# A top-k attention that feeds a mixture of experts: products moved inside the first 48 steps, and one row scaling a step

## The chip, the cores and the metric

The kernel runs on one core of a Trainium2 chip. The metric is the device time in microseconds (us) of one execution. PE is the matrix engine (TensorE), DVE the vector engine, ACT the scalar engine, POOL the GpSimd engine, SP the engine that issues most transfers. Each engine runs its own instructions strictly in order, and waits on the others by semaphores.

## What is computed

Eight batches of eight heads attend with 576 queries and keys of 64 numbers. In each row of scores only the 32 largest stay, the rest are masked. The rows of all heads (4608 x 512) then pass a mixture of eight experts, one expert to a token. All in float32; cut to what matters here:

```python
scores = scale * q @ k.T
kth = np.partition(scores, -32, axis=-1)[..., -32:-31]
scores = np.where(scores >= kth, scores, -1e9)
attn = np.exp(scores - scores.max(-1)); attn /= attn.sum(-1) + 1e-09
x = (attn @ v)                      # 4608 tokens x 512
e = argmax(x @ w_gate)              # one expert a token
out = gate_w * eom[e] * (relu(x @ w1[e]) @ w2[e])
```

## The kernel before

Attention is cut into 36 tiles of 128 queries and each tile into 4 steps of two heads: 144 steps. A step i is written as one pass of a loop (L873), and the order of the instructions on each engine is the order in which this loop writes them; nothing else sorts them. A pass works on several steps at once:

- PE: `scores(i+1)` (L275, into the PSUM tile `ps`), and the transposes of the exponentials of step i-2, `flip(i-2, part)` (L404, into PSUM tiles `pst`). A step has nine blocks of 128 columns. Part 0 is the first four (head 0), part 1 the fifth, which holds columns of both heads, part 2 the last four (head 1). `attend` (L436) multiplies them with the values, two steps at a time, in even passes.
- DVE: `rank` (L309, L312) finds 24 of the largest of step i from candidates, `window` (L351) the next eight of step i-1, `gmax` (L302) the candidates of step i+1, `choose` (L362, L366) the 32nd largest of step i-1, and `weigh` (L378) masks the exponentials of its head 0.
- ACT: a copy of the scores from PSUM (L283), `below` (L336, two sign functions, one to a head, which need the end of `rank`), `unveil` (L394, the exponential of head 1 of step i-2), copies of the transposes from PSUM (L412), `exps` (L346, head 0 of step i), and `veil` (L385, a sign function that needs `less`, L366).
- POOL: two sums after `below` (L339), which give `window` its input one pass later, `shift` (L325), and one sum after `veil` (L388).

In the first 48 steps (`LONE`) head 1 is masked by ACT and POOL (`veil`, `unveil`), in the later ones by DVE. There also run the slots of the mixture of experts (L714, L729), and after the last step a tail has the rest of them. In the first 48 steps PE has little to do, and 12 transposes of the identity without any use (L895) are written into each pass.

Once in four steps, when a tile is complete, two side products go through `side_start`: `gates` (L466, L457) in the passes with i mod 4 = 3, `rows` (L475, L457) in those with i mod 4 = 0. They share the PSUM tile of part 1, and are copied out after it (L470, L460). `rows` puts two scalings of the tile's rows on a list (L479, POOL); `run_slow(SUMS, ...)` starts those of cost 0.6 as long as the budget `SUMS` of a pass lasts. Small operations of the routing and of the setup are handed out one by one by `fill` (in the first steps the constants, L146 to L152). A pass with i mod 4 = 0 is called class 0 below, and so on to class 3; `attend` is in classes 0 and 2.

The pool `ps_t` has two banks in turn, so that a new tile `pst` waits until the last tile but one has been copied out.

Of the kernel before, what the change touches and what calls it, by code (L numbers as in the profile page):

```python
# [10 lines left out]
F32 = mybir.dt.float32  # L11
# [5 lines left out]
ALU = mybir.AluOpType  # L17
# [6 lines left out]
P = 128  # L24
# [5 lines left out]
USUAL = 11  # L30


SUMS = 1.3
DMAS = 2.0

NLIST = 12
# [3 lines left out]
def tile_topk_attention_moe(  # L40
# [11 lines left out]
    nc = tc.nc  # L52
# [77 lines left out]
    def setup():  # L130
# [5 lines left out]
        def gates():  # L136
            for a in range(2):
# [8 lines left out]
        ops = [lambda: nc.gpsimd.memset(wg, 0.0), gates,  # L146
               lambda: nc.gpsimd.memset(ones, 1.0), lambda: nc.gpsimd.memset(ones_b, 1.0),
               iota(before, [[1, P]], 0, -1),
               lambda: nc.gpsimd.tensor_scalar(before, before, 0.0, None, op0=ALU.is_gt),
               lambda: nc.vector.tensor_copy(before_b, before),  # L150
               iota(first, [[-1, E]], E), iota(carry0, [[REG, E]]),
               lambda: nc.gpsimd.memset(first_row, 0.0),  # L152
               iota(slot_iota, [[1, MAXS], [0, E]], 1), iota(slot_off, [[P, MAXS]]),
# [31 lines left out]
    def run(exact, stack):  # L185
# [205 lines left out]
        def unveil(i):  # L391
            if lone(i, 1):
                t, hp = divmod(i, NHP)
                nc.scalar.activation(EP[i][:, 1, :], VE.pop(i), AF.Exp, bias=VV.pop(i)[0][:, 1, 32:33], scale=SCALE,  # L394
                                     accum_out=SM[t][:, 2 * hp + 1:2 * hp + 2])

        def flip(i, part, extra=None):

            pt = EP[i].rearrange("p a s -> p (a s)")
            c0, c1 = ((0, 4), (4, 5), (5, 9))[part]  # L400
            n = c1 - c0
            ps = ps_t.tile([P, 4, P], F32, name="pst")
            for c in range(c0, c1):
                nc.tensor.transpose(ps[:, c - c0, :], pt[:, c * P:(c + 1) * P], ident)  # L404
            ev = extra(ps) if extra else None
            x = wk.tile([P, n, P], F32, name=f"pT{n}", bufs=6 if n == 4 else 3)
            PTT.setdefault(i, []).append(x)
            if part == 2:
                del EP[i]

            def copies():
                nc.scalar.activation(x, ps[:, :n, :], AF.Copy)  # L412
                if ev:
                    ev()
            return copies
# [398 lines left out]
        def side_start():  # L814

            f = side.popleft() if side else None

            def start(ps):
                copies, use = f(ps)
                uses.append(use)  # L820
                return copies
            return f and start

        def side_use():
            if uses:
                fill(len(urgent))
                uses.pop()()
# [45 lines left out]
        for i in range(NSTEP + 4):  # L873
            t, hp = divmod(i, NHP)
            step[0] = i
            if i + 1 < NSTEP:
                scores(i + 1)()
            for r in range(3):
                if i < NSTEP:
# [6 lines left out]
            spent[0] = 0.0  # L886
            if i < NSTEP:
                below(i)
            if 2 <= i < NSTEP + 2:
                unveil(i - 2)  # L890
            if 2 <= i < LONE:

                idle = ps_m.tile([P, 4, P], F32, name="pm")
                for c in range(12):
                    nc.tensor.transpose(idle[:, c % 4, :], ident, ident)  # L895
            early, late = [], []
            if 4 <= i < NSTEP + 4 and i % 2 == 0:
                early.append(attend(i - 4))
            if 2 <= i < NSTEP + 2:
                early.append(flip(i - 2, 0))  # L900
                early.append(flip(i - 2, 1, side_start()))
            if i >= NSTEP + 2:
                extra = side_start()
                if extra:
                    early.append(extra(ps_t.tile([P, 4, P], F32, name="pst")))
# [5 lines left out]
            if ev:  # L911
                late.append(ev)
            if 2 <= i < NSTEP + 2:
                late.append(flip(i - 2, 2))
            ev = turn_ahead() if room else None
            if ev:
                late.append(ev)
# [18 lines left out]
            run_slow(DMAS, ("ids", "out"))  # L936
            if 1 <= i <= NSTEP:
                veil(i - 1)
            side_use()
            fill(3)  # L940
            if i < NSTEP:
# [185 lines left out]
```

## Time and profile before

| | us |
|---|---|
| median of three runs (1297.45 to 1298.43) | 1297.87 |
| the profiled execution | 1299.58 |
| its span, first to last instruction | 1297.8 |
| steps 2 to 47 (22.70 to 342.71 of the span) | 320.0 |
| the later steps (342.71 to 1048.48) | 705.8 |
| the rest | 249.3 |

The profiled execution is 1.71 us above the median of the runs, and 1.8 us of its time lie outside the span. Stretches of the span are told by their start and end in us. A class is recognised in the trace by what follows: L475 marks class 0, L466 class 3. A step begins with the first L309 after L378.

### The profile page before, as it was taken

The numbers are of one execution on the slowest core, as the hardware profiler recorded it, in microseconds if no ns is written. First come the engines' busy times: TensorE is split into PE (matmuls) and PEld (weight loads), VectorE is DVE, ScalarE is ACT, GpSimd is POOL, SyncE is SP. The second block draws the span as 40 slices with busy tenths as digits, with TensorE's granted clock in tenths as the row PEclk, the third lists the DMA queues.
The fourth block names the chain that finished last, engine by engine and source line by source line (L and its number), as shares of the span: only waits on it lengthen the run. The fifth ranks groups of instructions, "written<-read, shape, count | busy, mean of one in ns | idle before, by whom it ended". The sixth has DMA issues, their size and how long they took to land.

```text
span 1297.8 us, 32273 instructions
## 1 busy us (share of the span) xinstructions
PE 1210.1 (93%) x10348; PEld 940.7 (72%) x10348; DVE 1143.7 (88%) x6113; ACT 984.5 (76%) x1928; POOL 758.2 (58%) x1221
## 2 busy tenths in 40 slices
PE   5887888887699999999999999999999999999996
PEld 4665665666577777777777777777777777999995
DVE  6999999999999999999999999999999963544443
ACT  5999998899887888888788787888887853454442
POOL 5666666588776766757667667567657733212110
PEclk7999999999999999999999999999999999999998
DMA  5400220021825654765456566755554467999990
GB/s 135 76 18 18 55 69 17 18 54 55 292 96 168 234 168 171 252 211 169 170 168 196 198 236 174 235 181 200 179 171 147 163 226 275 390 363 340 361 339 22
DMA packets 109387, 227.54 MB, mean 175 GB/s; under 512 B 14858, under 2 KB 33546, under 8 KB 108176
## 3 DMA queue, kind: packets, MB, share of 16 engines
q1 hardware_dynamic: 99536, 205.67, 47.6%
q0 software_dynamic: 7552, 18.96, 4.4%
q8 instruction: 86, 1.41, 0.5%
q10 hardware_dynamic: 2112, 0.68, 0.3%
q14 instruction: 101, 0.83, 0.2%
HBM read 206.68 MB, written 20.69 MB: 175 GB/s over the span
## 4 chain that ended last, share of the span: by engine, by line
PE 57%; DVE 24%; issue 14%; POOL 3%; ACT 1%; POOLq 0%; ACTq 0%
PE pm L714 14%; PE pm L729 13%; PE po L436 9%; PE ps L275 9%; PE pst L404 9%; DVE cand L302 8%; DVE v L351 5%; DVE cand L312 3%; DVE v L309 3%; DVE ep L378 2%; DVE x L362 2%; PE pst L457 1%; POOL xg L693 1%; PE pst L703 1%; PE pst L466 1%
## 5 line engine op out<-in xcount | busy, mean ns | idle before, releaser
L339 POOL TENSOR_TENSOR w<-s,marks 128x576 f32<-128x576 f32 x288 | 363.3, 1283 | 172.9 <-ACT marks L336 162.7
L302 DVE MAX8 cand<-s 128x8 f32<-128x72 f32 x2304 | 322.3, 222 | 8.7 <-ACT s L283 8.7
L714 PE MATMUL pm<-xs,w1t 128*128 128x128 f32 x2560 | 296.8, 275 | 0.9 <-issue 0.8
L714 PEld LDWEIGHTS pm<-xs,w1t 128*128 128x128 f32 x2560 | 292.0, 192 | 2.4 <-issue 1.1
L404 PE MATMUL pst<-ident,ep 128*128 128x128 f32 x1296 | 208.1, 285 | 68.7 <-ACT ep L394 56.2
L404 PEld LDWEIGHTS pst<-ident,ep 128*128 128x128 f32 x1296 | 148.6, 143 | 138.7 <-ACT ep L394 62.8
L336 ACT ACTIVATE marks<-s,v 128x576 int8<-128x576 f32 x288 | 220.9, 771 | 30.5 <-DVE v L309 27.2
L412 ACT ACTIVATE pT<-pst 128x512 f32<-128x512 f32 (+1 forms) x432 | 196.2, 484 | 17.0 <-PE pst L457 8.7
L351 DVE MAX8 v<-w 128x8 f32<-128x576 f32 x288 | 202.3, 745 | 0.0
L283 ACT ACTIVATE s<-ps 128x1152 f32<-128x1152 f32 (+1 forms) x145 | 163.2, 1126 | 51.5 <-PE ps L275 48.2
L275 PE MATMUL ps<-kst,qst 64*128 64x288 f32 (+1 forms) x1280 | 186.7, 442 | 5.4 <-ACT s L283 5.4
L378 DVE SCALAR_TENSOR_TENSOR ep<-s,kth,ep 128x576 f32<-128x576 f32 x240 | 188.7, 815 | 0.0
L436 PE MATMUL po<-pT,v 128*64 128x128 f32 (+3 forms) x3200 | 185.7, 267 | 0.1
L436 PEld LDWEIGHTS po<-pT,v 128*64 128x64 f32 (+1 forms) x3200 | 158.2, 136 | 33.8 <-issue 32.2
L729 PE MATMUL pm<-w2t,ht 128*128 128x512 f32 x400 | 180.4, 594 | 0.0
L346 ACT ACTIVATE ep<-s,v 128x576 f32<-128x576 f32 x240 | 176.1, 781 | 0.0
L740 POOL DMA_INDIRECT out_dram<-y,idt x40 | 49.8, 1246 | 190.9 <-ACT y L736 173.9
L309 DVE MAX8 v<-cand 128x8 f32<-128x64 f32 x864 | 148.4, 214 | 0.0
L275 PEld LDWEIGHTS ps<-kst,qst 64*128 64x128 f32 (+1 forms) x1280 | 100.7, 182 | 48.6 <-issue 25.1
L729 PEld LDWEIGHTS pm<-w2t,ht 128*128 128x128 f32 x400 | 72.2, 190 | 72.4 <-issue 72.4
L312 DVE MATCH_REPLACE8 cand<-v,cand 128x64 f32<-128x64 f32 x576 | 116.2, 210 | 0.0
L388 POOL TENSOR_TENSOR w<-s,marks 128x576 f32<-128x576 f32 x48 | 61.6, 1284 | 77.7 <-ACT marks L385 77.6
(166 smaller groups left out, 1520.9 us busy)
## 6 DMA issues: line engine op xcount, KB each, us to landing
w1t<-in_w_dram SPq DMA_DIRECT2D x40, 2048.0 KB
w2t<-in_w_dram SPq DMA_DIRECT2D x40, 2048.0 KB
v<-in_va_dram SPq DMA_DIRECT2D x8, 1152.0 KB
x_rows<-xu SPq DMA_DIRECT2D x36, 256.0 KB
qst<-in_qa_dram SPq DMA_DIRECT2D x70, 128.0 KB
kst<-in_ka_dram SPq DMA_DIRECT2D x14, 576.0 KB
ids<-far SPq DMA_DIRECT2D x1, 678.0 KB
xg<-x_rows,idt POOLq DMA_INDIRECT x40
```

What stands on the lines that cost most here:

```text
L275: nc.tensor.matmul(ps[qs, a, n, :288], Q[t][rows, hp, qs], K[b][rows, hp, cols], start=True, stop=True)
L302: nc.vector.max(out=c[:, 8 * g:8 * g + 8], in_=SC[i, a][:, g * GW:(g + 1) * GW])
L309: nc.vector.max(out=vs[:, a, 8 * r:8 * r + 8], in_=cs[a])
L336: nc.scalar.activation(m.bitcast(I8).rearrange("p (s b) -> p s b", b=2)[:, :, 1], s, AF.Sign, bias=vs[:, a, PIVOT - 1:PIVOT], scale=-(1.0 ...
L339: nc.gpsimd.tensor_tensor(w, s, m, op=ALU.add)
L351: nc.vector.max(out=VV[i][0][:, a, 24:32], in_=SW[i][0][a])
L378: nc.vector.scalar_tensor_tensor(e, SC.pop((i, a)), kth_col(i, a), e, op0=ALU.is_ge, op1=ALU.mult, accum_out=SM[t][:, 2 * hp + a:2 * hp + ...
L404: nc.tensor.transpose(ps[:, c - c0, :], pt[:, c * P:(c + 1) * P], ident)
L412: nc.scalar.activation(x, ps[:, :n, :], AF.Copy)
L436: nc.tensor.matmul(po[a * 64:(a + 1) * 64, k, qs], lhs, rhs, start=half and not k and not m, stop=(c == 3 and k == 1 and m == len(TT[t]) - 1))
L714: nc.tensor.matmul(ph[:, f - f0, :], w[:, c, f * P:(f + 1) * P], XS[s][:, c, :], start=(c == 0), stop=(c == NC - 1))
L729: nc.tensor.matmul(PY[s], HT[s][:, f, :], w[:, f, :], start=(f == 0), stop=(f == NF - 1))
```

## The change

In passes below 48 (`calm`), apart from a second version of the program for ties, which is not taken with these inputs:

- the scores are computed two steps ahead, not one: PE does them between part 1 and part 2 of the transposes, and ACT copies them after `veil`, at the end of the pass, ahead of the copy of part 2, which also moves there;
- part 0 is transposed first, and its copy stands ahead of `unveil`; then the side products, into the tile `mid`, in which part 1 later takes the first block; then `attend`, the 12 idle transposes, part 1, the scores, part 2.

In all passes the budget `SUMS` is 0.7, which lets one scaling of rows start in a pass, not two. In the setup, POOL writes the constant `before_b` itself, and a conversion on DVE goes.

```diff
-SUMS = 1.3
+SUMS = 0.7
 DMAS = 2.0
...
                iota(before, [[1, P]], 0, -1),
-               lambda: nc.gpsimd.tensor_scalar(before, before, 0.0, None, op0=ALU.is_gt),
-               lambda: nc.vector.tensor_copy(before_b, before),
+               lambda: nc.gpsimd.tensor_scalar(before_b, before, 0.0, None, op0=ALU.is_gt),
                iota(first, [[-1, E]], E), iota(carry0, [[REG, E]]),
                lambda: nc.gpsimd.memset(first_row, 0.0),
...
-        def flip(i, part, extra=None):
+        def flip(i, part, extra=None, bank=None):
             pt = EP[i].rearrange("p a s -> p (a s)")
             c0, c1 = ((0, 4), (4, 5), (5, 9))[part]
             n = c1 - c0
-            ps = ps_t.tile([P, 4, P], F32, name="pst")
+            ps = bank or ps_t.tile([P, 4, P], F32, name="pst")
             for c in range(c0, c1):
                 nc.tensor.transpose(ps[:, c - c0, :], pt[:, c * P:(c + 1) * P], ident)
-            ev = extra(ps) if extra else None
+            ev = extra(ps) if extra and not bank else extra
             x = wk.tile([P, n, P], F32, name=f"pT{n}", bufs=6 if n == 4 else 3)
             PTT.setdefault(i, []).append(x)
...
         for i in range(NSTEP + 4):
             t, hp = divmod(i, NHP)
             step[0] = i
-            if i + 1 < NSTEP:
+            if i + 1 < NSTEP and (i + 1, 0) not in SC:
                 scores(i + 1)()
             for r in range(3):
                 if i < NSTEP:
...
             spent[0] = 0.0
             if i < NSTEP:
                 below(i)
+            early, late, last = [], [], []
+            calm = i < LONE and not exact
+            mid = None
+            if calm and 2 <= i:
+                first_copy = flip(i - 2, 0)
+                mid = ps_t.tile([P, 4, P], F32, name="pst")
+                f = side_start()
+                beside = f(mid) if f else None
+                first_copy()
             if 2 <= i < NSTEP + 2:
                 unveil(i - 2)
+            if 4 <= i < NSTEP + 4 and i % 2 == 0:
+                early.append(attend(i - 4))
             if 2 <= i < LONE:
                 idle = ps_m.tile([P, 4, P], F32, name="pm")
                 for c in range(12):
                     nc.tensor.transpose(idle[:, c % 4, :], ident, ident)
-            early, late = [], []
-            if 4 <= i < NSTEP + 4 and i % 2 == 0:
-                early.append(attend(i - 4))
-            if 2 <= i < NSTEP + 2:
+            if mid is not None:
+                early.append(flip(i - 2, 1, beside, mid))
+            elif 2 <= i < NSTEP + 2:
                 early.append(flip(i - 2, 0))
                 early.append(flip(i - 2, 1, side_start()))
+            if calm and i + 2 < NSTEP:
+                last.append(scores(i + 2))
             if i >= NSTEP + 2:
...
             if 2 <= i < NSTEP + 2:
-                late.append(flip(i - 2, 2))
+                (last if calm else late).append(flip(i - 2, 2))
...
             run_slow(DMAS, ("ids", "out"))
             if 1 <= i <= NSTEP:
                 veil(i - 1)
+            for f in last:
+                f()
             side_use()
             fill(3)
             if i < NSTEP:
```

On ACT, the pass of class 0 with i = 8, before (from the copy of the scores of step 9 to `veil` of step 7):

```order
L283 ACTIVATE s<-ps 128x1152
L336 ACTIVATE marks_80,n<-s,v_920 128x576
L336 ACTIVATE marks_81,n<-s,v_920 128x576
L394 ACTIVATE ep,sums<-w,v_699 128x576
L438 ACTIVATE xT<-po 128x256
L412 ACTIVATE pT_1017<-pst 128x512
L412 ACTIVATE pT_1023<-pst 128x128
L460 ACTIVATE xu<-pst 128x256
L346 ACTIVATE ep<-s,v_920 128x576
L412 ACTIVATE pT_1029<-pst 128x512
L385 ACTIVATE marks_82<-s,less 128x576
```

and now, from `below` of step 8 to the copy of part 2:

```order
L335 ACTIVATE marks_80,n<-s,v_924 128x576
L335 ACTIVATE marks_81,n<-s,v_924 128x576
L412 ACTIVATE pT_980<-pst 128x512
L393 ACTIVATE ep,sums<-w,v_703 128x576
L438 ACTIVATE xT<-po 128x256
L412 ACTIVATE pT_1023<-pst 128x128
L460 ACTIVATE xu<-pst 128x256
L345 ACTIVATE ep<-s,v_924 128x576
L384 ACTIVATE marks_82<-s,less 128x576
L282 ACTIVATE s<-ps 128x1152
L412 ACTIVATE pT_1035<-pst 128x512
```

The copy of the scores went from the head of the pass to its end, the first copy of part 0 (128x512) from behind the exponential of head 1 (L394, now L393) to ahead of it, and the second (part 2) from ahead of `veil` (L385, now L384) to the very end.

On PE, two passes of class 2 and 3 before, up to the scores and the idle transposes of the pass of class 0 (`ps` are scores, `pm` the idle transposes, `ep` parts of the exponentials):

```order
L404 MATMUL pst<-ident,ep 128x128 x9
L275 MATMUL ps<-kst,qst 128x288 x4
L895 MATMUL pm<-ident 128x128 x12
L404 MATMUL pst<-ident,ep 128x128 x5
L466 MATMUL pst<-xT,wg 32x128 x4
L457 MATMUL pst<-ident,xT 128x128 x2
L404 MATMUL pst<-ident,ep 128x128 x4
L275 MATMUL ps<-kst,qst 128x288 x4
L895 MATMUL pm<-ident 128x128 x12
```

and now, from the idle transposes of class 2 to the side product `rows` of class 0 and the start of `attend`:

```order
L908 MATMUL pm<-ident 128x128 x12
L404 MATMUL pst<-ident,ep 128x128
L274 MATMUL ps<-kst,qst 128x288 x4
L404 MATMUL pst<-ident,ep 128x128 x8
L466 MATMUL pst<-xT,wg 32x128 x4
L457 MATMUL pst<-ident,xT 128x128 x2
L908 MATMUL pm<-ident 128x128 x12
L404 MATMUL pst<-ident,ep 128x128
L274 MATMUL ps<-kst,qst 128x288 x4
L404 MATMUL pst<-ident,ep 128x128 x8
L475 MATMUL pst<-ident,lt 128x128
L457 MATMUL pst<-ident,xT 128x128 x2
L436 MATMUL po<-pT_1238,v 64x128 x2
```

The side products moved from behind part 1 to ahead of the idle transposes, and `rows` (L475) stands ahead of `attend` (L436), which was ahead of all transposes of `ep`. Behind `attend` follow now:

```order
L436 MATMUL po<-pT_917,v 64x128
L908 MATMUL pm<-ident 128x128 x12
L404 MATMUL pst<-ident,ep 128x128
L274 MATMUL ps<-kst,qst 128x288 x4
L404 MATMUL pst<-ident,ep 128x128 x8
```

(the last matmul of `attend` in the pass with i = 8, the idle transposes, part 1, the scores of step 10, part 2 and part 0 of the next pass). In this pass L475 waits for the copy of part 2 of the pass ahead, whose bank `mid` gets.

On DVE, pass 1 before, where the constant is converted:

```order
L366 TENSOR_SCALAR less<-kth 128x1
L378 SCALAR_TENSOR_TENSOR ep,sums<-s,kth,ep 128x576
L150 CAST before_b<-before 128x128
L309 MAX v_283<-cand 128x8 x2
L312 MATCH_REPLACE cand<-v_283,cand 128x64 x2
```

and now:

```order
L365 TENSOR_SCALAR less<-kth 128x1
L377 SCALAR_TENSOR_TENSOR ep,sums<-s,kth,ep 128x576
L308 MAX v_289<-cand 128x8 x2
L311 MATCH_REPLACE cand<-v_289,cand 128x64 x2
L308 MAX v_289<-cand 128x8 x2
```

The conversion L150 is gone, and the first L309 of step 2 follows L378 (now L377).

## Rows read from the trace of the kernel before

**Rows 1.** The page, part 1: busy time of each engine, share of the span and instructions.

```profile
PE 1210.1 (93%) x10348; PEld 940.7 (72%) x10348; DVE 1143.7 (88%) x6113; ACT 984.5 (76%) x1928; POOL 758.2 (58%) x1221
```

**Rows 2.** Busy time of the engines in two stretches, steps 2 to 47 and the later steps: length, then PE, weight loads, DVE, ACT, POOL, granted clock as a share of the full one, share of the DMA engines, GB/s.

```profile
22.70:342.71 320.01, 259.72 (x2448) 197.02 (x2450) 317.45 (x1866) 287.42 (x607) 218.64 (x313) 0.95 0.20 56
342.71:1048.48 705.77, 700.31 (x6145) 522.31 (x6142) 704.38 (x4011) 580.23 (x1182) 473.83 (x809) 0.99 0.57 188
```

**Rows 3.** The chain of waits by line, in 150 to 190 us (steps 21 to 25) and in 400 to 1000 us (later steps).

```profile
by line: DVE cand L302 29.6%; DVE v L351 20.8%; DVE cand L312 11.7%; DVE ep L378 11.4%; DVE v L309 10.7%; DVE x L362 10.4%; DVE lg L494 1.8%; DVE less L366 1.7%; DVE tl L492 1.1%; issue 0.6%; DVE r L502 0.3%; DVE r L501 0.2%
...
by line: PE pm L714 23.9%; PE pm L729 23.0%; PE po L436 17.1%; PE ps L275 15.8%; PE pst L404 15.3%; PE pst L457 2.0%; PE pst L703 1.5%; PE pst L466 1.2%; PE pst L475 0.4%; PE pst L539 0.1%; issue 0.0%
```

**Rows 4.** Three stretches with the busy time of the instructions of L362 alone (`choose`): length, busy DVE time and number of instructions, granted clock, DMA share, GB/s. The first is six groups of four steps (8 to 31), the second steps 24 to 27, the third steps 28 to 31.

```profile
61.83:226.74 164.91, 19.12 (x96) 0.97 0.12 35
172.19:198.97 26.78, 2.54 (x16) 1.00 0.20 65
198.97:226.74 27.77, 3.55 (x16) 0.94 0.06 20
```

**Rows 5.** DVE in order of time: `choose` (L362) in step 22, its first instruction and the last read of its sum, and its first instruction in steps 24 and 25.

```profile
164.59 0.22 DVE L362 SCALAR_TENSOR_TENSOR x<-left,n,v 128x8 f32<-128x8 f32 x1
...
164.89 0.08 DVE L362 DVE_READ_ACCUMULATOR x<-left,n,v 128x1 f32 x1
...
177.23 0.82 DVE L362 SCALAR_TENSOR_TENSOR x<-left,n,v 128x8 f32<-128x8 f32 x1
...
184.67 0.68 DVE L362 SCALAR_TENSOR_TENSOR x<-left,n,v 128x8 f32<-128x8 f32 x1
```

**Rows 6.** ACT in order of time, step 23 (class 3) into step 24 (class 0): start, duration, engine, instruction.

```profile
167.57 0.78 ACT L336 ACTIVATE marks<-s,v 128x576 int8<-128x576 f32 x1
...
169.10 0.76 ACT L394 ACTIVATE ep<-w,v 128x576 f32<-128x576 f32 x1
...
169.86 0.57 ACT L412 ACTIVATE pT<-pst 128x512 f32<-128x512 f32 x1
171.10 0.28 ACT L412 ACTIVATE pT<-pst 128x128 f32<-128x128 f32 x1 [0.67 <-PE pst L457]
171.27 0.27 ACT L470 ACTIVATE lt<-pst 128x128 f32<-128x128 f32 x1
171.43 0.39 ACT L460 ACTIVATE xu<-pst 128x256 f32<-128x256 f32 x1
171.69 0.79 ACT L346 ACTIVATE ep<-s,v 128x576 f32<-128x576 f32 x1
172.36 0.61 ACT L412 ACTIVATE pT<-pst 128x512 f32<-128x512 f32 x1
172.83 0.80 ACT L385 ACTIVATE marks<-s,less 128x576 int8<-128x576 f32 x1
173.50 1.15 ACT L283 ACTIVATE s<-ps 128x1152 f32<-128x1152 f32 x1
174.51 0.81 ACT L336 ACTIVATE marks<-s,v 128x576 int8<-128x576 f32 x1
```

**Rows 7.** PE in order of time: part 1 and the end of the side product `gates` in step 23 (class 3), then step 24 (class 0).

```profile
170.01 0.33 PE L404 MATMUL pst<-ident,ep 128*128 128x128 f32 x1 [1.86 <-ACT ep L394]
...
170.62 0.44 PE L457 MATMUL pst<-ident,xT 128*128 128x128 f32 x2
...
172.60 1.53 PE L895 MATMUL pm<-ident 128*128 128x128 f32 x12
174.06 2.55 PE L436 MATMUL po<-pT,v 64*64 64x128 f32 x40
176.54 0.77 PE L404 MATMUL pst<-ident,ep 128*128 128x128 f32 x5
177.14 0.27 PE L475 MATMUL pst<-ident,lt 128*128 128x128 f32 x1
```

**Rows 8.** POOL in order of time: the two sums of `below` in step 24, then the two scalings and the two sums in step 25 (class 1).

```profile
175.49 2.53 POOL L339 TENSOR_TENSOR w<-s,marks 128x576 f32<-128x576 f32 x2 [0.24 <-ACT marks L336]
...
181.67 1.18 POOL L479 TENSOR_TENSOR xu<-xu,r 128x256 f32<-128x256 f32 x2
182.81 2.52 POOL L339 TENSOR_TENSOR w<-s,marks 128x576 f32<-128x576 f32 x2
```

**Rows 9.** Busy time in two stretches, from part 1 of step 23 (class 3) and of step 29 (class 1) on; columns as in Rows 2.

```profile
170.01:172.60 2.59, 2.59 (x24) 1.62 (x24) 2.56 (x19) 1.93 (x6) 1.16 (x2) 1.00 0.00 0
210.48:213.12 2.64, 2.63 (x11) 1.73 (x13) 2.61 (x16) 2.38 (x5) 1.75 (x3) 0.50 0.26 99
```

**Rows 10.** PE in order of time in step 29: part 0, then part 1 and part 2.

```profile
207.78 0.60 PE L404 MATMUL pst<-ident,ep 128*128 128x128 f32 x4
210.46 1.59 PE L404 MATMUL pst<-ident,ep 128*128 128x128 f32 x5 [2.08 <-ACT ep L394]
```

**Rows 11.** POOL and DVE in order of time where step 2 begins.

```profile
21.96 0.56 POOL L149 TENSOR_SCALAR before<-before 128x128 f32<-128x128 f32 x1
...
22.55 0.23 DVE L150 CAST before_b<-before 128x128 bf16<-128x128 f32 x1 [2.06 <-POOL before L149]
22.70 0.35 DVE L309 MAX8 v<-cand 128x8 f32<-128x64 f32 x2
...
23.44 0.73 POOL L133 IOTA slot_iota<- 1x344 f32 x1
```

## The prediction

> **What bounds the kernel now.** I read the page first. DVE is busy for 88% of the span, PE for 93% [rows 1], but these are means over unlike stages, so the table by stretches comes next. In steps 2 to 47, which the change rewrites, DVE works 317.5 of 320.0 us and PE only 259.7, a fifth of it idle transposes; in the later steps PE works 700.3 of 705.8 [rows 2]. The chain of waits says the same: in steps 21 to 25 every piece of it is DVE, in the later steps every piece is PE [rows 3]. So what the change does to ACT and PE in the first 48 steps can only pay where DVE itself is held up.
>
> It is held up in one line. `choose` (L362) takes 0.22 us and the pair with its last read 0.38 when nothing is in the way, but 0.82 in step 24 and 0.68 in step 25 [rows 5]. Both end when POOL's two sums L339 end: 177.23 + 0.82 = 178.05 against 175.49 + 2.53 = 178.02, and 185.35 against 185.33 [rows 5, 8]. So DVE stands still, inside an instruction that counts as busy, until POOL has finished. Four pairs would be 1.52 us; steps 8 to 31 have 19.12 / 6 = 3.19 in four steps, so 1.67 of the 164.91 / 6 = 27.49 us of four steps are stall, and DVE's own work is 25.8 [rows 4]. In steps 24 to 27, at full clock, four steps took 26.78; in 28 to 31, at a mean clock of 0.94, 27.77 [rows 4]. A stretch at half clock (1.2 of 2.4 GHz) costs about 1.0 us there, since nothing else is unlike.
>
> L339 is late for two reasons. In class 0, ACT's first sign function is late (L339 had waited for it [rows 8]), because the class 3 ahead lost 0.67 us waiting for the side product before it could copy part 1 [rows 6]. In class 1 the two scalings stand on POOL ahead of the sums: they end at 182.85, and the sums begin at 182.81 [rows 8].
>
> **Part by part. The chain on ACT.** With copies and sign functions in another order, I add up ACT from one first sign function (L336) to the next, starts to starts from [rows 6]: the two sign functions 1.53; copy of part 0 0.48 (172.36 to 172.83); `unveil`; `exps` 0.67; `veil` 0.67; copy of the scores 1.01; copy of part 2 0.48. What is new is the piece from `unveil` to the copy of part 1. Part 1 holds columns of head 1, so PE can transpose only when `unveil` has written: it begins at 170.01, 0.91 behind the start of `unveil` at 169.10, and takes 0.33 [rows 6, 7]; the copy follows a few hundredths behind PE (171.10 after 171.06). That makes 1.27. Before, the copy of part 0 stood in this hole and hid it (169.10 + 0.76 + 0.48 = 1.24); now it stands ahead of `unveil`, and the hole is open, for 0.51 us in each step without `attend`'s copy.
>
> - Classes 1 and 2: 1.53 + 0.48 + 1.27 + 0.17 (copy of part 1) + 0.67 + 0.67 + 1.01 + 0.48 = 6.28 us.
> - Class 3 adds the two copies of `gates`, 0.16 + 0.26: 6.70. Before it was 174.51 - 167.57 = 6.94, so having the side product out of the way of part 1 is worth 0.24 net.
> - Class 0: the added wait. L475 (`rows`) goes into the bank that the copy of part 2 of the pass ahead empties, and that copy is now the last thing on ACT before the sign function: it starts 0.48 before it and takes 0.6, so L475 starts 0.12 behind the sign function. Queued behind it on PE are `rows` itself (about 0.4, from the end of `gates` and L457 in steps 23 and 24), `attend` 176.54 - 174.06 = 2.48, the idle transposes 174.06 - 172.60 = 1.46 and part 1 0.33 [rows 7]. The copy of part 1 comes at 0.12 + 0.4 + 2.48 + 1.46 + 0.37 = 4.83 instead of 1.53 + 0.48 + 1.27 = 3.28, and everything on ACT waits for it. Then 0.17 + 0.26 + 0.67 + 0.67 + 1.01 + 0.48 = 3.26: 8.09.
>
> Four steps: 2 x 6.28 + 6.70 + 8.09 = 27.35 us. That is above DVE's own 25.8, so ACT, with PE's queue in class 0, becomes the bound, and the stall of `choose` stays at about 27.35 - 25.8 = 1.6 in four steps, moved into class 1 (about 1.2) and class 0 (0.4). Compared with clean steps before (26.78) this is worse by 0.6, compared with the mean (27.49) it is the same.
>
> **The clock.** In step 29 PE sat idle for 2.08 us between part 0 and part 1, and the clock granted from there on was 0.50; in step 23 it sat idle for 1.86, and the clock was 1.00 [rows 7, 9, 10]. After the change class 1 is the step with the long hole: part 0 and the idle transposes are done early, and part 1 waits for a sign function that is 1.3 us late. I estimate 2.7 us, longer than any of these, and so a fall in 6 or 7 of 10 groups. A fall costs 0.6 (between 0.15, the slower part 1 alone, and the 1.0 of [rows 4]): 0.4 in four steps. The Trainium skill, "TensorE: Matmul & The Clock Gate", section "HAM oscillation — how this bites in real kernels", describes a kernel whose matrix work between two waits is shorter than the wait, and which starts every piece cold. [...]
>
> So four steps: 27.75 against 27.49, +0.27. Eight groups of steps 8 to 47 pay it (in the two with the routing, its extra DVE work hides the late sums): **+2.1 us**.
>
> **The constant.** DVE's conversion L150 waits 2.06 us for POOL and delays step 2 by 2.06 + 0.15 = 2.2 [rows 11]. It goes. What is late next is POOL: L149 still starts at 21.96, and 0.56, slot_iota's 0.73 and some small operations stand ahead of the sums of step 2, which comes 2.2 earlier now. That gives back 0.6; some of step 3's stall may go as well. Between -2.2 and -1.0, I take **-2.0**.
>
> **The end of the calm steps.** Step 48 finds its successor's scores done: one scores product less on PE, where PE begins to bound, and a copy of 1.01 less on ACT. Between -1.0 and 0: **-0.5**.
>
> **SUMS.** One scaling less ahead of the sums in class 1 would be worth the 0.46 of [rows 5], but there the sign function is now later than both scalings would end; nothing. The second goes to class 2, where POOL has no sums before the sign function; nothing. Its store to x_rows goes down SP's queue one pass later; the gathers that read it come only after the routing, several passes later. In the later steps PE is the chain [rows 3] and hides POOL's order; -0.5 to +0.5.
>
> **Sum.** 2.1 - 2.0 - 0.5 = -0.4 us, against the profiled execution (1299.58, which is 1.7 above the median of the runs) and so as well against the median: 1297.87 - 0.4 = **1297.5**. The difference to the time before is smaller than what a measurement can tell from no change (0.2%, 2.6 us).
>
> **Rivals.** *The clock falls in every group.* Place: class 1, between the idle transposes and part 1; it decides if half clock follows that hole every time, at its full price. Then 27.35 + 1.0 = 28.35, 8 x 0.86 = +6.9 - 2.5 = +4.4: 1302.3. For it: step 29 fell at 2.08. Against it: step 23 kept the clock at 1.86. [...] Chance 0.24, slower. *The clock holds and the start gains all,* because PE's work is spread better in classes 2, 3 and 0: 8 x (27.35 - 27.49) - 2.2 - 1.0 = -4.3: 1293.6. For it: the product in class 3 now breaks up the hole there. Chance 0.2, faster. *The wait of L475 does not count,* because the copy of part 2 comes early enough: the four steps fall to DVE's own 25.8, 8 x -1.7 - 2.5 = -16: 1282. Against it is ACT's order, in which that copy is the last. Chance 0.08, faster.
>
> **How the numbers follow.** The forecast, a trade inside 1295.3 to 1300.4, has 0.48 of the chance. Faster by over 0.2%: 0.2 + 0.08 = 0.28; slower 0.24. The range from 1292.5 to 1303 takes in the first two rivals and leaves out the third and the outer edge of the slower one, some 0.16.
>
> **What the profile after would show.** Right: no wait of DVE for L149; in class 0 a wait of ACT of over 1 us for part 1 behind `attend`; on PE, L475 waiting for the copy of part 2; in each step without `attend` a wait of about half a us of ACT for part 1; `choose` longest in class 1; four steps at 27.4 to 28.4; the later steps as long as before to half a us. Wrong, if `choose` no longer stalls in class 1 (then the third rival), if four steps take over 28.5, or if the later steps change by more than 1 us, which nothing here accounts for.

## The result, and the profile of the changed kernel

The changed kernel takes 1310.74 us (median of 4 runs, 1309.68 to 1312.15), the kernel before 1297.66 us beside it: a ratio of 1.0099, 95% interval 1.0079 to 1.0118. It is slower by 13 us, and the prediction (1297.5, range 1292.5 to 1303.0) was wrong.

The profiled execution took 1312.15 us, 12.57 more than that of before. Line numbers are one lower now up to L387 (choose is L361, the sums are L338, L387 and the sign functions L335, L384), L895 is L908, and L492 and L501 kept theirs. The first view is the busy time by stretch, steps 2 to 47 and the later steps, with the columns of [rows 2]; the second is `choose` alone, with those of [rows 4], in steps 8 to 31, 8 to 11 and 16 to 19.

```profile
21.01:355.79 334.78, 262.57 (x2467) 202.75 (x2468) 324.23 (x1867) 286.57 (x609) 220.79 (x316) 0.94 0.19 50
355.79:1060.61 704.82, 699.98 (x6141) 522.44 (x6140) 703.12 (x4009) 580.39 (x1182) 473.41 (x809) 0.99 0.57 191
```

```profile
60.26:234.27 174.01, 21.54 (x96) 0.94 0.12 33
60.26:88.61 28.35, 2.18 (x16) 1.00 0.07 20
117.22:147.27 30.05, 4.55 (x16) 0.89 0.25 58
```

Step 2 starts 1.69 earlier (21.01 against 22.70), steps 2 to 47 are 14.77 longer, the later steps 0.95 shorter and the rest 0.44 longer: +12.57. So all of the loss is in the first steps. Four steps take 29.07 on the mean of eight groups (steps 8 to 31 and 36 to 43; in the kernel before 27.48). `choose` holds only 21.54 - 19.12 = 2.4 of the 9.1 us by which steps 8 to 31 grew [rows 4]; the rest must be elsewhere. Three places show it.

**Class 0: DVE waits for the side product.** The views are PE in order of time from step 12 (class 0) into step 13, the same for ACT at part 1, and the list of DVE's waits in steps 2 to 47 (engine, line, what it waited for: us, times, longest).

```profile
90.88 0.33 PE L475 MATMUL pst<-ident,lt 128*128 128x128 f32 x1 [1.41 <-ACT pT L412]
91.05 0.38 PE L457 MATMUL pst<-ident,xT 128*128 128x128 f32 x2
91.36 2.55 PE L436 MATMUL po<-pT,v 64*64 64x128 f32 x40
93.84 1.53 PE L908 MATMUL pm<-ident 128*128 128x128 f32 x12
95.21 0.27 PE L404 MATMUL pst<-ident,ep 128*128 128x128 f32 x1
...
97.51 1.47 PE L908 MATMUL pm<-ident 128*128 128x128 f32 x12
101.70 0.33 PE L404 MATMUL pst<-ident,ep 128*128 128x128 f32 x1 [2.72 <-ACT ep L393]
```

```profile
95.52 0.28 ACT L412 ACTIVATE pT<-pst 128x128 f32<-128x128 f32 x1 [1.17 <-PE pst L404]
95.69 0.38 ACT L460 ACTIVATE xu<-pst 128x256 f32<-128x256 f32 x1
```

```profile
DVE tl L492 <- ACT xu L460: 7.9, 10, 0.9
DVE cand L301 <- ACT s L282: 0.6, 2, 0.4
```

L475 waits for the copy of part 2, `attend` and the idle transposes stand behind it, and part 1 comes last, as the prediction had it. But the copies behind part 1 have a second reader: `use` of `rows` (L492) on DVE waits for L460 in class 0 itself, 0.8 to 0.9 us in each of ten groups.

**Class 1: the hole, and half clock behind it.** The last row on PE above shows the hole: 2.72 us, the estimate was 2.7. Half clock follows in each group from step 12 on, in 9 of the 10 of steps 8 to 47. In steps 18 and 19, PE, a stretch by engine (columns of [rows 2]), then ACT, POOL and DVE:

```profile
130.59 0.47 PE L404 MATMUL pst<-ident,ep 128*128 128x128 f32 x1 [2.76 <-ACT ep L393]
130.99 2.20 PE L274 MATMUL ps<-kst,qst 64*64 64x288 f32 x16
133.12 1.97 PE L404 MATMUL pst<-ident,ep 128*128 128x128 f32 x8
135.02 3.31 PE L436 MATMUL po<-pT,v 64*64 64x128 f32 x40
```

```profile
132.50:136.70 4.20, 4.20 (x30) 2.92 (x24) 4.20 (x28) 3.65 (x8) 3.03 (x4) 0.50 0.17 63
```

```profile
139.94 0.28 ACT L412 ACTIVATE pT<-pst 128x128 f32<-128x128 f32 x1 [1.17 <-PE pst L404]
...
143.88 2.52 POOL L338 TENSOR_TENSOR w<-s,marks 128x576 f32<-128x576 f32 x2 [0.73 <-ACT marks L335]
...
145.12 1.30 DVE L361 SCALAR_TENSOR_TENSOR x<-left,n,v 128x8 f32<-128x8 f32 x1
```

The scores, part 2 and `attend` of class 2 run slowly (3.31 instead of 2.55), the copy of part 1 of class 2 waits 1.17, so the sums of class 3 end at 146.40 and `choose` stands still until then. The mean stall of `choose` is now 0.46, 0.30, 0.49 and 0.90 in classes 0 to 3 (before 0.69, 0.55, 0.16, 0.29).

**Class 3: an addition stands still.** DVE and POOL in step 11, which had full clock:

```profile
81.75 1.27 POOL L387 TENSOR_TENSOR w<-s,marks 128x576 f32<-128x576 f32 x1 [1.43 <-ACT marks L384]
...
81.86 1.18 DVE L501 TENSOR_SCALAR r<-sums 128x8 f32<-128x8 f32 x1
82.96 0.34 DVE L308 MAX8 v<-cand 128x8 f32<-128x64 f32 x2
```

L501 adds 1e-9 to eight sums and takes 0.16 us; here it takes 1.18 and ends with L387 of POOL (83.02). Nothing that it reads comes from POOL. This happened in 4 of the 11 tiles in steps 2 to 47 (3.4 us). Before, POOL's sum did not begin earlier than L501 in any but the last of them. The change moved `veil` ahead of two copies, and behind a class 2 at full clock POOL's sum now begins 0.1 to 0.2 us before L501.

The constant: DVE no longer waits for L149, but step 2 comes earlier than POOL can serve it. POOL in order of time:

```profile
22.57 0.56 POOL L149 TENSOR_SCALAR before_b<-before 128x128 bf16<-128x128 f32 x1
...
23.50 0.73 POOL L133 IOTA slot_iota<- 1x344 f32 x1
...
24.35 2.50 POOL L338 TENSOR_TENSOR w<-s,marks 128x576 f32<-128x576 f32 x2
```

### The profile page after: what moved, and what is told of

The parts are those of the page before. It is cut to its first block, busy times and chain, and to the rows that moved or that the text cites. A ratio compares the mean times of both kernels' runs of the same rounds, so it can differ in the third digit from the quotient of the medians.

```text
span 1310.4 us, 32257 instructions
## 1 busy us (share of the span) xinstructions
PE 1210.6 (92%) x10348; PEld 944.5 (72%) x10348; DVE 1148.9 (88%) x6112; ACT 982.8 (75%) x1928; POOL 758.3 (58%) x1221
## 4 chain that ended last, share of the span: by engine, by line
PE 59%; DVE 21%; issue 14%; ACT 3%; POOL 2%; POOLq 0%; ACTq 0%
PE pm L714 14%; PE pm L729 13%; PE po L436 11%; PE pst L404 8%; PE ps L274 8%; DVE cand L301 6%; DVE v L350 4%; DVE cand L311 3%; DVE v L308 3%; DVE ep L377 2%; DVE x L361 2%; PE pst L457 1%; PE pm L908 1%; POOL xg L693 1%; PE pst L703 1%
## 5 line engine op out<-in xcount | busy, mean ns | idle before, releaser
L338 POOL TENSOR_TENSOR w<-s,marks 128x576 f32<-128x576 f32 x288 | 363.3, 1283 | 179.5 <-ACT marks L335 169.8
L404 PEld LDWEIGHTS pst<-ident,ep 128*128 128x128 f32 x1296 | 151.3, 145 | 135.5 <-ACT ep L393 55.9
L335 ACT ACTIVATE marks<-s,v 128x576 int8<-128x576 f32 x288 | 221.1, 774 | 31.6 <-DVE v L308 29.8
L412 ACT ACTIVATE pT<-pst 128x512 f32<-128x512 f32 (+1 forms) x432 | 199.9, 486 | 37.9 <-PE pst L404 35.0
L436 PE MATMUL po<-pT,v 128*64 128x128 f32 (+3 forms) x3200 | 189.3, 270 | 0.0
L377 DVE SCALAR_TENSOR_TENSOR ep<-s,kth,ep 128x576 f32<-128x576 f32 x240 | 188.4, 814 | 0.3 <-issue 0.3
L436 PEld LDWEIGHTS po<-pT,v 128*64 128x64 f32 (+1 forms) x3200 | 161.2, 138 | 34.7 <-issue 33.0
L387 POOL TENSOR_TENSOR w<-s,marks 128x576 f32<-128x576 f32 x48 | 61.5, 1280 | 83.8 <-ACT marks L384 83.8
```

The costliest lines, as they stand in the source:

```text
L335: nc.scalar.activation(m.bitcast(I8).rearrange("p (s b) -> p s b", b=2)[:, :, 1], s, AF.Sign, bias=vs[:, a, PIVOT - 1:PIVOT], scale=-(1.0 ...
L338: nc.gpsimd.tensor_tensor(w, s, m, op=ALU.add)
L377: nc.vector.scalar_tensor_tensor(e, SC.pop((i, a)), kth_col(i, a), e, op0=ALU.is_ge, op1=ALU.mult, accum_out=SM[t][:, 2 * hp + a:2 * hp + ...
L436: nc.tensor.matmul(po[a * 64:(a + 1) * 64, k, qs], lhs, rhs, start=half and not k and not m, stop=(c == 3 and k == 1 and m == len(TT[t]) - 1))
```

## The experiments

Twelve kernels. "Group" is the mean length of four steps in the same eight groups; each ratio is to runs of the kernel before on the same chip (its medians there 1298.98, 1299.19 and 1298.67). A profile is of one run: those of e4, e5 and e10 are of their fastest, those of e2, e6 and the kernel after of their slowest, so that lengths of steps and groups compare less exactly than the times.

| | edit | us | ratio, 95% interval | steps 2-47 | group |
|---|---|---|---|---|---|
| before | | 1297.66 | | 320.0 | 27.48 |
| after | | 1310.74 | 1.0079 to 1.0118 | 334.8 | 29.07 |
| e10 | after, hole of class 1 filled | 1306.11 | 1.0044 to 1.0075 | 326.8 | 28.13 |
| e5 | after, classes 1 and 3 filled | 1306.52 | 1.0038 to 1.0078 | 328.7 | 28.36 |
| e4 | after, `rows` back | 1299.99 | 0.9994 to 1.0021 | 319.6 | 27.41 |
| e3 | after, both products back | 1318.85 | 1.0112 to 1.0172 | 342.0 | 30.01 |
| e6 | after, no L501 | 1297.56 | 0.9973 to 0.9996 | 327.5 | 28.48 |
| e11 | before, no L501 | 1292.87 | 0.9943 to 0.9970 | 318.5 | 27.55 |
| e8 | before, `choose` of one source | 1296.66 | 0.9976 to 0.9997 | 318.0 | 27.51 |
| e7 | e4 and e5 | 1293.36 | 0.9936 to 0.9969 | 316.5 | 27.16 |
| e9 | e4, e5 and e6 | 1288.52 | 0.9900 to 0.9933 | 314.7 | 27.06 |
| e12 | e4, e6 and e10 | 1281.51 | 0.9854 to 0.9884 | 306.4 | 26.28 |
| e1 | before, the constant alone | 1297.88 | 0.9973 to 0.9998 | 321.6 | 27.48 |
| e2 | before, `SUMS` alone | 1295.94 | 0.9971 to 0.9991 | 319.0 | 27.47 |

### The clock: e5 and e10

```diff
-                for c in range(12):
+                for c in range(28 if i % 2 else 12):
```

> The kernel after (1310.7), with 28 idle transposes instead of 12 in the odd steps, so that PE has some 1.9 us more of work in the hole of class 1 (2.7 us) and of class 3. Theory 1, the clock: half clock follows this hole in every group of four steps and costs the better part of the loss; with the hole filled the granted clock stays at 1.00 in steps 12 to 47, four steps fall from 29.1 to about 28.0, and the time to 1301 to 1304. Theory 2, the order itself: ACT is late in class 0 because the side product rows waits for the copy of part 2 and stands ahead of attend, whatever the clock; then the clock rises and the time stays at 1308 to 1311.

In e10 the condition is `i % 4 == 1`.

> The kernel after with 28 idle transposes in class 1 alone, the step with the 2.7 us hole; class 3 keeps its 12. It parts the clock from the two other losses. Theory: the clock stays full, and every group of four steps is as long as the one group of the kernel after that had no half clock (steps 8 to 11, 28.35 us, with L501 standing still and the wait in class 0): 28.0 to 28.4, the steps 2 to 47 fall from 334.8 to 327 to 330, the time to 1303 to 1306. Rival, that the clock is only a sign of a late ACT and costs nothing by itself: 1309 to 1311.

PE in step 17 of e10 (25 of the 28 transposes stand in the first row), and a stretch from within step 6 to the end of step 43:

```profile
126.33 2.89 PE L908 MATMUL pm<-ident 128*128 128x128 f32 x25
130.23 0.33 PE L404 MATMUL pst<-ident,ep 128*128 128x128 f32 x1 [1.01 <-ACT ep L393]
130.49 1.20 PE L274 MATMUL ps<-kst,qst 64*64 64x288 f32 x16
```

```profile
48.70:316.70 268.00, 219.34 (x2233) 174.27 (x2229) 259.24 (x1521) 234.49 (x503) 175.47 (x234) 1.00 0.13 38
```

The granted clock is 1.00 throughout, and `choose` loses 0.02 us in classes 2 and 3 (after: 0.49 and 0.90). Work without any use, put on an engine that waits, shortens steps 2 to 47 by 8.0 us: the clock is a cause, not a sign. The 8.0 are what is left after L501, which at full clock stands still in 9 tiles and not in 4 (8.5 us and not 3.4). The medians are only 4.6 us apart, since the profiles compare the fastest run of e10 (1303.72) with the slowest of the kernel after (1312.15). e10 ends just above its range; e5, with class 3 filled as well, is no better and ends 2.5 above its own, which did not count the further stalls of L501.

### `rows` ahead of `attend`: e3 and e4

e4 puts the product of class 0 behind part 1 again, e3 both products.

```diff
                 first_copy = flip(i - 2, 0)
-                mid = ps_t.tile([P, 4, P], F32, name="pst")
-                f = side_start()
-                beside = f(mid) if f else None
+                mid = True
+                if i % 4 == 3:
+                    mid = ps_t.tile([P, 4, P], F32, name="pst")
+                    f = side_start()
+                    beside = f(mid) if f else None
                 first_copy()
...
-            if mid is not None:
+            if mid is True:
+                early.append(flip(i - 2, 1, side_start()))
+            elif mid is not None:
                 early.append(flip(i - 2, 1, beside, mid))
```

(e3 leaves out the four lines of `if i % 4 == 3`, and the `elif` with them.)

> The kernel after, with only the product of class 0 (rows) behind part 1 again; gates of class 3 stays ahead of the idle transposes. Theory 2, the wait of rows: this one move carries the loss, and gates ahead of part 1 is worth the 0.24 us in a group that the prediction gave it: 2 us better than with both products back, 1294 to 1297. Theory 1, the clock: the hole of class 1 stays and half clock with it, 1302 to 1307.

> The kernel after, with both side products (gates and rows) behind part 1 of the transposes again, as before the change; part 0 first, the scores two steps ahead and the late copy of part 2 stay. Theory 1, the clock: the hole in class 1 comes from part 0 and the idle transposes being done early, and that stays; half clock stays in most groups, 1304 to 1308. Theory 2, the wait of rows: with the product behind part 1 nothing on PE waits for the copy of part 2 ahead of attend, ACT is not late out of class 0, DVE no longer waits 0.8 us in L492 in class 0, and the hole in class 1 is shorter by about 1.3 us as well; four steps at 27.5, and 1296 to 1299.

PE in step 12 of e4 (class 0; it starts at 87.17), where L475 stands behind part 1 and waits for nothing:

```profile
92.18 0.33 PE L404 MATMUL pst<-ident,ep 128*128 128x128 f32 x1 [0.20 <-ACT ep L393]
92.35 0.27 PE L475 MATMUL pst<-ident,lt 128*128 128x128 f32 x1
```

Part 1 comes 5.0 behind the start of the step instead of 6.6, the 7.9 us of L492 are gone, class 0 is 7.27 instead of 8.24, and the kernel is level with the one before: this one move takes back 12 of the 13 us. e4 ended between what the two theories gave: the hole of class 1 is still there (2.72), and the scores behind it ran at half clock in 4 of the 9 groups of steps 8 to 43.

e3 fell the other way: 19 us slower than e4. My theory of the order missed what `gates` ahead of part 1 is worth. PE in step 15 (class 3) of e3, and the clock there:

```profile
118.45 0.47 PE L404 MATMUL pst<-ident,ep 128*128 128x128 f32 x1 [2.48 <-ACT ep L393]
118.85 0.66 PE L466 MATMUL pst<-xT,wg 128*32 128x128 f32 x8
```

```profile
118.40:124.00 5.60, 5.55 (x35) 3.04 (x35) 5.07 (x27) 3.72 (x8) 2.20 (x4) 0.50 0.00 0
```

Without `gates` in it, class 3 has a hole as well (2.44 to 2.48, once 3.45; with `gates` 1.0 to 1.9), half clock follows it in 7 of 9 groups, and class 0 behind it takes 9.46 us. So `gates` ahead is worth 30.01 - 27.41 = 2.6 us a group in these two profiles by its place in the hole, not 0.24.

### L501, and what a stalled instruction of DVE waits for: e6, e8 and e11

```diff
-            urgent.append(lambda: nc.vector.tensor_scalar(r, sm, 1e-9, None, op0=ALU.add))
-            urgent.append(lambda: nc.vector.reciprocal(r, r))
+            urgent.append(lambda: nc.vector.reciprocal(r, sm))
```

> The kernel after without the one addition of 1e-9 to the row sums (L501, one tensor_scalar of DVE in each tile); the reciprocal takes the sums as they are. Left out: that addition. In the kernel after L501 took 0.66 to 1.84 in step 11 and ended when POOL's L387 ended (1.81); four of them lasted 0.8 us too long, 3.4 in all. Theory, a lock: this instruction and POOL's cannot run at the same time, and it goes with the instruction; the steps 2 to 47 shrink by 3 to 3.4 us, the time is 1307 to 1308. Rival: what is late is POOL's sum, and the next instruction of DVE or the choice one step later loses the same: 1310 to 1311.

> The kernel before (1297.7) without L501 (the addition of 1e-9 to the row sums is left out). Of the 13 us that this gave in the kernel after, 7.2 were in steps 2 to 47 and about 5.5 behind the last step, where the routing of the last tiles came a pass earlier. In the kernel before L501 stood still once, for 0.55 us. If what stands in its way is the collision: 0.5 to 1 us in steps 2 to 47, and 5 to 6 behind the last step, 1291 to 1292.5. Rival, that the stretch behind the last step depends on the order of this change: 1297.

e6 gave 13 us, not 3. In the profiles steps 2 to 47 shrank by 7.2 and what lies behind the last step by 5.8, and the later steps took 1.7 more. The reciprocal, in the same place and at the same time as POOL's sum (0.66 to 0.85 in step 11, L387 from 0.54 to 1.81), does not stand still, so the stall goes with the instruction. Of the 7.2 us the stall itself was 3.4. The rest goes with the clock: the mean granted clock is 0.973 to 0.976 in the four runs of the kernel after and 0.979 to 0.986 in the ten of e6. Why it is higher without L501 stays open. Where L501 stands still, PE's hole ahead of part 1 in class 3 is 1.65 and not 0.65, but that alone does not bring half clock on in the class 1 behind it: in e4 that class ran at full clock behind each of the five stalls of steps 7, 11, 15, 19 and 35, and fell to half behind each of the five tiles (steps 23, 27, 31, 39, 43) in which L501 did not stand still. Two groups of e6, `choose` alone, steps 8 to 11 at full clock and steps 20 to 23 with a stretch at half clock (of the eight, the first three are like the one and the last five like the other):

```profile
58.85:86.20 27.35, 2.26 (x16) 1.00 0.07 21
141.05:170.04 28.99, 3.62 (x16) 0.94 0.06 20
```

In e11, which ends 0.4 above its range, the 5.6 us behind the last step come as well (243.7 instead of 249.3), and steps 2 to 47 give 1.5. The routing of the last tiles starts at 1069.4 there and at 1077.0 in the kernel before, one step earlier: these operations are handed out one by one, and there is one fewer. That part has nothing to do with the change. Set beside each other, the two kernels without L501 say more: their ratios to the kernel before are 0.9984 (e6) and 0.9956 (e11), so without this addition the change costs 0.28%, 3.6 us (give or take 2), and not 13. Some 9 of the 13 us came in with it.

```diff
-                nc.vector.scalar_tensor_tensor(x, left, n[:, a:a + 1], vs[:, a, 24:32], op0=ALU.is_equal,
-                                               op1=ALU.mult, accum_out=kth_col(i, a))
+                nc.vector.tensor_reduce(kth_col(i, a), vs[:, a, 24:32], axis=AX.X, op=ALU.min)
```

> The kernel before (1297.7), with the choice of the 32nd largest (L362, which reads two tiles in SBUF) replaced by the smallest of the eight values of the window, which reads one. Left out: the case that the 24th and 25th value of a row agree to 2 in a million, for which L362 is there. It tells what DVE stands still for there. Theory 1, a lock: an instruction of DVE that reads two tiles in SBUF and POOL's sums exclude each other; the smallest does not stand still, but L378 right behind it reads two tiles as well and stands still in its place until the sums L339 end; the time stays at 1296 to 1298. Theory 2, a wait for data: the smallest stands still as L362 did, and L378 does not; the time is the same. Theory 3, the stall belonged to this instruction alone: steps 2 to 47 lose some 15 of the 17.8 us, 1281 to 1284.

POOL and DVE in step 24 of e8 (compare [rows 5, 8]; `weigh` is L377 here):

```profile
175.69 2.52 POOL L339 TENSOR_TENSOR w<-s,marks 128x576 f32<-128x576 f32 x2 [0.25 <-ACT marks L336]
178.15 0.73 POOL L367 COPY near<-v 128x4 f32<-128x4 f32 x1
...
177.06 0.21 DVE L362 TENSOR_REDUCE kth<-v 128x1 f32<-128x8 f32 x2
...
177.38 1.46 DVE L377 SCALAR_TENSOR_TENSOR ep<-s,kth,ep 128x576 f32<-128x576 f32 x1
```

Theory 1 holds. The operation of one source passes while POOL sums (none of 288 took over 0.163), and L377 behind it, which took at most 0.86 before, stands still in its place. In steps 2 to 47 it takes 1.19 on the mean instead of 0.81, 17.7 us more in 46 steps, as much as `choose` had lost there (35.03 - 46 x 0.38 = 17.5). The time hardly moves. The Trainium skill, "SBUF — State Buffer", section "Who interferes with whom", gives the rule: a VectorE instruction with two inputs in SBUF needs a port pair that a GpSimd instruction reading SBUF needs too, a `tensor_scalar` in one of its two-port modes needs it as well, and the one issued first keeps it to its end. These rows agree, L501 (1.18 against 0.16) and the copy L367 of POOL behind L377 (0.73 against 0.2) too. The ports, and the mode in which L501 ran, no run here shows.

### Together: e7, e9 and e12

> The kernel after with rows behind part 1 again and with 28 idle transposes instead of 12 in the odd steps (the two experiments in one). Theory: the two losses are separate. Rows behind part 1 alone took steps 2 to 47 from 334.8 to 319.6 us, with a half clock in 6 of 10 groups left; the groups without it took 25.95 to 27.3 us, those with it 27.6 to 28.9. With the hole filled all are at 26 to 27.3: steps 2 to 47 in 306 to 312 us, the time 1286 to 1292. Rival: the longer idle transposes delay part 1 in the odd steps, and what the clock gives is lost there: 1297 to 1300. A second loss that may grow, as it did with the hole filled alone (8.5 us in 9 steps): L501 against POOL's L387.

> The kernel after with rows behind part 1, 28 idle transposes in the odd steps, and without L501 (the addition of 1e-9 to the row sums is left out). If the three losses add up: 5 to 8 us less than with the first two alone, steps 2 to 47 in 300 to 305 us, and 1280 to 1285. Rival, that POOL's L387 holds up the next instruction of DVE in place of L501: as with the first two alone.

> The kernel after with rows behind part 1, without L501 (the addition of 1e-9 to the row sums is left out), and with 28 idle transposes in class 1 alone. In the run with 28 in both odd steps, part 1 of class 3 was copied 0.9 us late (5.96 instead of 5.07 behind the start of the step) and class 0 paid 1.1 us for it in choose. With class 3 as it was, four steps should take 25.9 to 26.2 instead of 27.07: steps 2 to 47 in 303 to 307 us instead of 314.7, the time 1278 to 1281 instead of 1288.5. Rival: the hole of class 3 then brings half clock in its place, and the time stays at 1286 to 1290.

e7 missed its range by 1.4: L501 stood still in 9 tiles (8.3 us). e9 gained 4.8 over it where 5 to 8 were expected, but 5.6 of it behind the last step; in steps 2 to 47 what L501 gave went into `choose` of class 0 (1.08 instead of 0.52), because part 1 of class 3 was late behind 28 idle transposes. e12 takes these out of class 3. Its steps 2 to 47 by engine, and L492 on DVE, the first instruction behind `weigh` in a class 0 (step 24):

```profile
20.88:327.32 306.44, 266.82 (x2654) 212.13 (x2654) 304.40 (x1860) 284.19 (x610) 222.79 (x319) 1.00 0.22 61
```

```profile
170.71 0.28 DVE L492 TENSOR_TENSOR tl<-pst,r 128x128 f32<-128x128 f32 x1
```

The clock is full, L492 waits for nothing, and a group takes 26.28, close to DVE's own 25.8. At 1281.51 us, half a us above its range, e12 beats both kernels: 17 us below the one before, and 11 below the one before without L501 (1292.87), which is what the change is worth once its three costs are gone. Leaving L501 out loses nothing: the row's maximum is subtracted, so the largest exponential is about 1, and in float32 a sum of 1 or more does not change by 1e-9.

### The small parts: e1 and e2

```diff
-               lambda: nc.gpsimd.tensor_scalar(before, before, 0.0, None, op0=ALU.is_gt),
-               lambda: nc.vector.tensor_copy(before_b, before),
+               lambda: nc.gpsimd.tensor_scalar(before_b, before, 0.0, None, op0=ALU.is_gt),
```

> The kernel before (1297.7) with the constant alone: POOL writes before_b itself, no conversion on DVE. Step 2 started 1.7 us earlier in the kernel after, and stalled 0.6 in it. If nothing later takes it back: 1296.0 to 1296.6. If the steps behind it are bound by something that does not come earlier (rival): 1297.7.

```diff
-SUMS = 1.3
+SUMS = 0.7
```

> The kernel before (1297.7) with SUMS 0.7 alone: one scaling of rows (L479) a pass instead of two. The prediction gave it nothing in the kernel after, because the sign function would be late there. In the kernel before, the two scalings of class 1 stand ahead of the sums and choose lost 0.55 us a step in class 1: with one fewer, 0.3 to 0.55 in each of ten groups, 1292.5 to 1295. Rival: the stall of class 1 is the late sign function, not the scalings, or the second scaling holds up POOL in class 2: 1297 to 1299.

The constant alone is worth 1.9 us by its ratio (0.3 to 3.5), near what was expected. `SUMS` alone is worth 2.5 (1.2 to 3.8), just short of the 2.7 expected at least: the stall of class 1 goes from 0.55 to 0.01 as expected, but classes 2 and 3 take back 0.33 and 0.21, so that a group is as long as before; in the profile 1.0 us is gained in steps 2 to 47 and 1.75 in the later steps. Why the later steps gain was not tried.

## Why the prediction was wrong, point by point

**The chain on ACT** (27.35 in four steps) was right, as a sum and in each class. e6, which has neither L501 nor, in steps 8 to 15, half clock, takes 27.34 and 27.35. ACT in e6, the first sign function of steps 8 to 12:

```profile
61.02 0.81 ACT L335 ACTIVATE marks<-s,v 128x576 int8<-128x576 f32 x1
...
69.10 0.80 ACT L335 ACTIVATE marks<-s,v 128x576 int8<-128x576 f32 x1
...
75.39 0.78 ACT L335 ACTIVATE marks<-s,v 128x576 int8<-128x576 f32 x1
...
81.67 0.78 ACT L335 ACTIVATE marks<-s,v 128x576 int8<-128x576 f32 x1
...
88.37 0.81 ACT L335 ACTIVATE marks<-s,v 128x576 int8<-128x576 f32 x1
```

From start to start that is 8.08, 6.29, 6.28 and 6.70 against the 8.09, 6.28, 6.28 and 6.70 that were added up. e10, at full clock, takes 28.13, and L501 stood still for 1.02 in 6 of its 8 groups: 28.13 - 0.77 = 27.36. What was wrong is where DVE pays: the detour of class 0 was charged to `choose` in class 1 (1.2, measured 0.30), while L492, a reader of the same copies, paid it in class 0. Without that detour the group takes 26.28 (e12), so the wait of L475 costs 1.1.

**The clock** is the term that failed. The place and the hole were right (2.72 for 2.7). The number of falls was low: 6 or 7 of 10, and it was 9 of 10, every group from step 12 on. The price was far too low: 0.6, between 0.15 and the 1.0 of [rows 4]. The seven of the eight groups with half clock took 28.31 to 30.28, on the mean 29.18: 29.18 - 27.35 = 1.8 each, so 7 x 1.83 / 8 = 1.6 in a group where the prediction had 0.4. In e6, where L501 cannot blur it, five of eight took 28.73 to 29.95, 1.4 to 2.6 more than 27.35. The 1.0 was measured where half clock lay over another order of work: now scores, part 2 and `attend` of class 2 lie in it. That the price is higher because ACT has no slack behind them is argued; no run parts it. The slower rival had the mechanism, at 1.0 in every group, and falls short by the price.

**L501** was not in the prediction at all. Of the eight groups it stood still in one, 1.02: 0.13 in a group. But some 9 of the 13 us go away when it is left out of both kernels (e6, e11), more than its stalls add up to, and how it goes with the lower clock is not shown. And at full clock, where the change would have been worth something, it stood still in 6 of 8 (e10), so that it would have taken the gain in any case. The prediction saw DVE stand still inside `choose` until POOL's sums ended, and did not ask which other instructions of DVE would do so, and which of POOL's were moved.

So 27.35 + 1.6 + 0.13 = 29.08, the measured 29.07, and 8 x (29.07 - 27.48) = 12.7 of the 14.8 us. The other 2.0 are the group of steps 32 to 35 (31.77 against 29.73), whose routing was supposed to hide the late sums.

**The other terms** were near, as far as they can be told: step 2 started 1.7 earlier by the constant, for -2.0 (in the other profiles it started at 19.8 to 21.2 with the edit and at 22.8 to 23.0 without). The later steps took 0.95 less, for -0.5 by the end of the calm steps; but with `SUMS` alone they took 1.75 less (e2), and in the profiles of the changed kernel and e3, e4, e5, e7 and e10 they took 704.2 to 705.9, so that this term is not shown. `SUMS` at nothing was too little by some 2 us for the kernel before; what it gives in the changed kernel was not tried.

**What was to be seen:** the wait of L475 and the wait of ACT for part 1 in class 0 came as told. `choose` is longest in class 3, not in class 1, and four steps took over 28.5, which the prediction had named as the sign of its failure.

The Trainium skill, "TensorE: Matmul & The Clock Gate", section "HAM oscillation — how this bites in real kernels", describes a kernel whose matrix work between two waits is shorter than the wait. That is not the case here: ahead of the hole of 2.72 us in step 13 PE had worked from 90.88 to 98.98, 8.1 us. Half clock followed such holes in most groups, and not in all: after a hole of 2.72 to 2.76 steps 8 to 11 of the kernel after and steps 8 to 19 of e6 stayed at full clock.

## What to carry to other kernels

When a transfer or a product is moved ahead, follow every reader of the copies that come later for it, on all engines, not only the next link of the chain that was summed. When DVE is seen to stand still inside an instruction while POOL works, list all instructions of that kind (two SBUF inputs, `tensor_scalar`), and see where the change puts POOL's long ones beside them: here a 0.16 us addition cost 1 us each time by a shift of a tenth. And price a half-clock stretch by the work that will lie in it and the slack behind it, not by a stretch elsewhere; if PE waits anyway, idle matmuls in the hole are the cheap test.

## What the runs showed of the hardware

Idle transposes are not free cover: 16 more of them in class 1 kept the clock at 1.00 for 268 us and gave 8.0 us in steps 2 to 47, and the same 16 in class 3 cost 0.8 us a group, 0.65 of it in class 0 (e9 against e12). The same program runs at different clocks from one execution to the next: the ten runs of e6 go from 1293.98 at a mean granted clock of 0.986 to 1300.31 at 0.979, while the four of e12, whose profile has no hole of 2.7 us, lie within 1.1 us.
